# First tiles of a spectral-mixing kernel in pieces of 256 columns, the second K tile in three passes, eight warm-up products instead of nine

## The chip, the core and the metric

The kernel runs on one core of a Trainium2 chip. The metric is the device time of one execution in microseconds (us): the median before is 1849.59 us over three runs (1849.43, 1849.59 and 1850.13). Lower is better.

## What is computed

A Fourier mixing of x along both dimensions (real part only) and a token-mixing MLP on a layer-normed x are joined by a gate per token. All tensors are float32.

```python
# x: (1, 2048, 1024); DFT matrices 2048x2048 and 1024x1024, real and imaginary; F = 3584
g = sigmoid((x * gate_w).sum(-1, keepdims=True))
p, q = einsum("bsd,ed->bse", x, dft_hid_re), einsum("bsd,ed->bse", x, dft_hid_im)
a = einsum("ts,bse->bte", dft_seq_re, p) - einsum("ts,bse->bte", dft_seq_im, q)
h = layernorm(x)                                   # over the 1024 channels
u = gelu(einsum("bsd,sf->bdf", h, w1) + b1)
b = (einsum("bdf,fs->bds", u, w2) + b2).transpose(0, 2, 1)
out = g * a + (1 - g) * b
```

## The kernel before

**Stages.** Four stages follow each other, each a large matrix product: `Fourier` (names q_...), `Mixed` (y_...), `Up` (u_...) and `Down` (o_...). Each is a bilinear scheme of 26 block products, a table of plus and minus signs that says which blocks are added up before a product and where the product is added to. A block product j goes over K tiles of 128 rows. For K tile k there is a stationary tile W (q_W..., 128 rows of x by 512 columns in the first stage, 256 KB) and a moving tile R (q_R..., 128 rows of a DFT matrix by 1024 columns, 512 KB). For `Fourier` there are 4 K tiles, taken in groups of 1, 1 and 2 (`Q_TAKES`), and the product fills all eight PSUM banks: four 128-column blocks m of W by two 512-column halves n of R.

**Split operands.** Every operand is split into a rounded part `hi` (fp32r, a copy on ACT or DVE) and a rest `lo` (a subtraction on DVE), and three products stand for one: hi·hi, hi·lo and lo·hi. So one block product of `Fourier` is 4 K tiles x 8 banks x 3 = 96 matmuls of 128x128 by 128x512.

**Order.** Tasks (a load, a split, a group of matmuls, a copy out of PSUM) are entered in a `Graph`. `schedule` plays the program through with costs from a table (`HOP`, `ISSUE`, `dve`, `act`, `DMA_RATE`, `DMA_LATENCY`, and `FIRST_LATENCY` for loads whose key is below `FIRST_KEYS`), takes matmul tasks strictly in the order in which they were entered, and orders all others on ACT, DVE, SP and POOL by due time. It also picks the SBUF slot of each buffer. The program order that comes out is then fixed on every engine. A change of the costs can thus move instructions anywhere behind it, though never a matmul group before another.

**The head of the program.** The first block product (j = 0) starts from nothing. TensorE runs nine products of a constant (`warm_up`, line 1328 in the profile) while the first tiles come. In the text below W0, W1, W2, W3 and R0 to R3 are the tiles of K tiles 0 to 3 of this first block product. W0 is loaded by a DMA from ACT's queue, R0 in two halves of 512 columns and everything else from SP's queue (line 573 is the helper `load`). For K tile 0, `Fourier.split` makes W0's `hi` on ACT in two parts of 128 and 384 columns (line 990), R0's first half `hi` on DVE (line 998), W0's `lo` and the `lo` of R0's first half on DVE (line 1010), and the second half of R0 by the general helper (596 on ACT, 603 on DVE). `Fourier.matmuls` (line 1035) then goes pass by pass over four banks at a time: for n = 0 W hi·R hi, W lo·R hi, W hi·R lo, then the same for n = 1. K tile 1 and the pair of K tiles 2 and 3 use the general `Bilinear.matmuls` (lines 899, 900, 901), bank by bank: hi·hi, hi·lo and lo·hi of one bank before the next bank.

**The end.** The last bank's sum is added by DVE (line 943), stored by a DMA from SP, and the program ends when it has landed. A variant in which the last bank goes in two halves exists behind the switch `LAST_HALVES`, which is False.

Of the kernel before, what the change touches and what calls it, by code (L numbers as in the profile page):

```python
# [30 lines left out]
ISSUE = {"SP": 0.43, "ACT": 0.43, "POOL": 0.85}  # L31
DMA_RATE = 375e3
DMA_LATENCY = 5.5
FIRST_LATENCY = 2.7
FIRST_KEYS = 0.5
LANES = 8


# [214 lines left out]
Y_TAKES, U_TAKES, O_TAKES = (2, 2), (2, 2), (2, 1, 1, 1, 2)  # L253
Q_WIDE, Y_WIDE, O_WIDE = "", "WR", ""
Q_BEHIND = (1,)
QUARTERS = False
LAST_HALVES = False


class Buf:  # L260
# [85 lines left out]
class Graph:  # L346
# [3 lines left out]
    def add(self, engines, key, fn, r=(), w=(), nbytes=0):  # L350
        t = Task(len(self.tasks), key, engines, fn, nbytes)
        self.tasks.append(t)

        def parts(reg):
            b, p = reg if isinstance(reg, tuple) else (reg, None)
            t.bufs[b] = None
            return b, range(b.parts) if p is None else p if isinstance(p, tuple) else (p,)

        for reg in r:
            b, ps = parts(reg)  # L360
            for p in ps:
# [137 lines left out]
def gated_mix_kernel(  # L499
# [62 lines left out]
    def slot(n, name, dtype=F32):  # L562
        return View(Buf("f" if n > H else "h", name, None, 1, dtype), 0, n)
# [383 lines left out]
    class Fourier(Bilinear):  # L947
# [13 lines left out]

        def block(self, x_, b, j, k, key):

            if (j, k) != (0, 0):
                return super().block(x_, b, j, k, key)
            src, r = self.source(x_, b, k)
            if x_ == "W":
                b = Buf("h", f"q_W{b}_p0_0", None, 4)
                for c0, n, part in self.pieces(H):
                    load(-3, View(b, c0, n, part), src[:, c0:c0 + n], queue="ACT")  # L970
                return View(b, 0, H)
            b = Buf("f", f"q_R{b}_p0_0", None, 4)
            for c0, n, part in self.pieces(H):
                load(-3, View(b, c0, n, tuple(p // 2 for p in part[::2])), src[:, c0:c0 + n])
            load(-2, View(b, H, H, (2, 3)), src[:, H:])
            return View(b, 0, D)
# [4 lines left out]

        def split(self, x_, key, v, j, k, negate):
            if (j, k) != (0, 0):
                return super().split(x_, key, v, j, k, negate)
            if x_ == "W":
                hi, lo = Buf("h", "q_p0_w_0_hi", None, 4, F32R), slot(H, "q_p0_w_0_lo", F32R)
                for c0, n in ((0, 2 * P), (2 * P, 2 * P)) if QUARTERS else ((0, P), (P, 3 * P)):
                    part = tuple(range(c0 // P, (c0 + n) // P))
                    c, src = View(hi, c0, n, part), View(v.buf, c0, n, part)
                    g.add({"ACT": act(n)}, key - 3, lambda e, c=c, src=src: nc.scalar.activation(  # L990
                        c.ap, src.ap, AF.Copy, scale=-1.0 if negate else 1.0), r=(src.reg,), w=(c.reg,))
                self.low(key - 3, v, View(hi, 0, H), lo, negate)
                return View(hi, 0, H), lo
            both = [Buf("f", f"q_p0_r_0_{p}", None, 4, F32R) for p in ("hi", "lo")]
            for c0, n, part in self.pieces(H):
                part = tuple(p // 2 for p in part[::2])
                hi, src = View(both[0], c0, n, part), View(v.buf, c0, n, part)
                g.add({"DVE": dve(n)}, key - 3, lambda e, hi=hi, src=src: nc.vector.tensor_scalar(
                    hi.ap, src.ap, -1.0 if negate else 1.0, None, op0=ALU.mult), r=(src.reg,), w=(hi.reg,))
            first, second = [[View(b, c, H, part) for b in (v.buf, *both)] for c, part in ((0, (0, 1)), (H, (2, 3)))]  # L1000
            self.low(key - 3, *first, negate)
            split_into(key - 2, *second, negate)
            return [View(b, 0, D) for b in both]
# [9 lines left out]

        def matmuls(self, j, ks, ops, eps):

            if j or ks != (0,):
                return super().matmuls(j, ks, ops, eps)
            (rh, rl), (wh, wl) = ops[0]
            for n in range(2):
                for m in range(4):  # L1020
                    self.PS[0, m, n] = View(Buf("ps", f"ps_q_p0_{m}_{n}"), 0, H)
# [137 lines left out]
    class Down(Bilinear):  # L1159
# [46 lines left out]
        def matmuls(self, j, ks, ops, eps):  # L1206
            if not (LAST_HALVES and j == len(self.out) - 1 and ks[-1] == self.nk - 1 and ks[0]):
                return super().matmuls(j, ks, ops, eps)
            self.nm -= 1
            super().matmuls(j, ks, ops, eps)  # L1210
            self.nm += 1
            m, old = self.nm - 1, self.PS[j % self.chains, self.nm - 1, 0]
            (q, coef), = self.reads[j]
            b = self.perm[0][q // 2] * 2 + self.perm[2][q % 2]
            o, key = self.C.pop((b, m, 0)), step + len(ks) + 1
            for h in range(2):
                c, bank = slice(h * H // 2, (h + 1) * H // 2), View(old.buf, h * H // 2, H // 2, (2 * h, 2 * h + 1))

                def go(_, c=c, bank=bank):
                    for i, ((rh, rl), (wh, wl)) in enumerate(ops):  # L1220
                        for w, r in ((wh, rh), (wh, rl), (wl, rh)):
                            nc.tensor.matmul(bank.ap, w.ap[:, m * P:(m + 1) * P], r.ap[:, c], start=False,
                                             stop=(i, w) == (len(ops) - 1, wl), skip_group_check=True)

                g.add({"PE": 0.36 * len(ops)}, step, go, r=[v.reg for x in ops for pair in x for v in pair], w=(bank.reg,))
                half = View(o.buf, o.c0 + h * H // 2, H // 2, (o.part[h],))
                self.accumulate(key, b, m, 0, half, bank, eps * coef)
                _, dst, _ = self.place(b, m)
                store(key, dst[:, c], None, half, "SP")

        def finish(self, key, b, m, n, o, j):
            _, dst, reg = self.place(b, m)
# [91 lines left out]

    def warm_up(_):
        ones = nc.const_aps.tensor(1.0, [P, H], mybir.dt.bfloat16)
        for n in range(9):
            nc.tensor.matmul(pw.t, ones[:, :P], ones, start=True, stop=True)  # L1328

    g.add({"PE": 4.0}, 0, warm_up, w=(pw,))  # L1330

    for st in (Fourier(), Mixed(), Up(), Down()):
        st.build()
# [61 lines left out]
```

## Time and profile before

| | us |
|---|---|
| median of three runs | 1849.59 |
| the profiled execution | 1849.4 |
| its span, first to last instruction | 1847.6 |
| TensorE matmul busy in the span | 1842.9 |
| DVE busy | 1692.4 |
| ACT busy | 875.2 |
| first matmul of the work starts at | 4.58 |
| last matmul starts at | 1843.38 |

The span begins with the first instruction that the profile holds; 1.8 us of the time of the execution lie outside it. Rows of the timeline read: start in us, duration in us, engine, line, operation, out<-in by names without numbers, tile, count, and in brackets the idle time before it with what ended it. PE is TensorE's matmul, PEld its weight load, SPq and ACTq the DMA issues of those queues. Matmuls are pipelined: the 0.39 us of one matmul overlap the next, so the distance between starts says what one costs.

### The profile page before, as it was taken

The numbers are of one execution on the slowest core, as the hardware profiler recorded it, in microseconds if no ns is written. First come the engines' busy times: TensorE is split into PE (matmuls) and PEld (weight loads), VectorE is DVE, ScalarE is ACT, GpSimd is POOL, SyncE is SP. The second block draws the span as 40 slices with busy tenths as digits, with TensorE's granted clock in tenths as the row PEclk, the third lists the DMA queues.
The fourth block names the chain that finished last, engine by engine and source line by source line (L and its number), as shares of the span: only waits on it lengthen the run. The fifth ranks groups of instructions, "written<-read, shape, count | busy, mean of one in ns | idle before, by whom it ended". The sixth has DMA issues, their size and how long they took to land.

```text
span 1847.6 us, 23997 instructions
## 1 busy us (share of the span) xinstructions
PE 1842.9 (100%) x8121; PEld 1524.0 (82%) x8121; DVE 1692.4 (92%) x2370; ACT 875.2 (47%) x1311; POOL 206.4 (11%) x355
## 2 busy tenths in 40 slices
PE   9999999999999999999999999999999999999999
PEld 7888888888888888888888888888888888888887
DVE  8999689989989999989889798879999999999995
ACT  5533334434344786597343344444654534444441
POOL 0100010111021001001121000001220000001111
PEclk9999999999999999999999999999999999999999
DMA  9978387969698887988677447667899666674963
GB/s 379 359 249 282 126 284 295 336 244 375 240 328 313 298 297 259 354 306 288 221 255 241 163 148 254 225 210 246 295 372 295 193 211 209 214 217 114 302 166 69
DMA packets 189451, 472.71 MB, mean 256 GB/s; under 512 B 23248, under 2 KB 23248, under 8 KB 189328
## 3 DMA queue, kind: packets, MB, share of 16 engines
q1 hardware_dynamic: 156240, 368.40, 58.3%
q0 software_dynamic: 32944, 102.52, 16.7%
q8 instruction: 63, 1.03, 0.2%
q14 instruction: 60, 0.49, 0.1%
q10 hardware_dynamic: 144, 0.26, 0.0%
HBM read 367.29 MB, written 103.81 MB: 255 GB/s over the span
## 4 chain that ended last, share of the span: by engine, by line
PE 100%; DVE 0%; issue 0%
PE ps_q_p L901 10%; PE ps_q_p L900 10%; PE ps_q_p L899 10%; PE ps_o_p L901 9%; PE ps_u_p L900 9%; PE ps_u_p L901 9%; PE ps_o_p L900 9%; PE ps_o_p L899 9%; PE ps_u_p L899 9%; PE ps_y_p L899 5%; PE ps_y_p L900 5%; PE ps_y_p L901 5%; PE ps_q_p L1035 0%; PE pw L1328 0%; DVE o_c L943 0%
## 5 line engine op out<-in xcount | busy, mean ns | idle before, releaser
L899 PE MATMUL ps_o_p<-o_p_r,o_p_w 128*128 128x512 f32 x728 | 283.2, 389 | 0.0
L900 PE MATMUL ps_o_p<-o_p_r,o_p_w 128*128 128x512 f32 x728 | 283.2, 389 | 0.0
L901 PE MATMUL ps_o_p<-o_p_r,o_p_w 128*128 128x512 f32 x728 | 283.2, 389 | 0.0
L900 PE MATMUL ps_u_p<-u_p_r_lo,u_p_w_hi 128*128 128x512 f32 x595 | 231.5, 389 | 0.0
L901 PE MATMUL ps_q_p<-q_p_r_hi,q_p_w_lo 128*128 128x512 f32 x576 | 224.1, 389 | 0.0
L899 PE MATMUL ps_u_p<-u_p_r_lo,u_p_w_hi 128*128 128x512 f32 x483 | 187.9, 389 | 0.0
L901 PE MATMUL ps_u_p<-u_p_r_lo,u_p_w_lo 128*128 128x512 f32 x483 | 187.9, 389 | 0.0
L596 ACT ACTIVATE q_p_r_hi<-q_R_p 128x1024 fp32r<-128x1024 f32 (+1 forms) x100 | 103.9, 1053 | 169.1 <-DVE q_R_p L566 87.3
L596 ACT ACTIVATE u_p_w_hi<-u_W_p 128x896 fp32r<-128x896 f32 x104 | 97.1, 950 | 150.4 <-DVE u_W_p L566 75.5
L899 PE MATMUL ps_q_p<-q_p_r_hi,q_p_w_lo 128*128 128x512 f32 x416 | 161.8, 389 | 0.0
L900 PE MATMUL ps_q_p<-q_p_r_lo,q_p_w_lo 128*128 128x512 f32 x416 | 161.8, 389 | 0.0
L900 PEld LDWEIGHTS ps_o_p<-o_p_r,o_p_w 128*128 128x128 f32 x728 | 136.7, 188 | 28.5
L899 PEld LDWEIGHTS ps_o_p<-o_p_r,o_p_w 128*128 128x128 f32 x728 | 136.7, 188 | 28.3
L901 PEld LDWEIGHTS ps_o_p<-o_p_r,o_p_w 128*128 128x128 f32 x728 | 136.7, 188 | 28.3
L899 PE MATMUL ps_q_p<-q_p_r_hi,q_p_w_hi 128*128 128x512 f32 x408 | 158.7, 389 | 0.0
L900 PE MATMUL ps_q_p<-q_p_r_lo,q_p_w_hi 128*128 128x512 f32 x408 | 158.7, 389 | 0.0
L603 DVE TENSOR_TENSOR q_p_r_lo<-q_R_p,q_p_r_hi 128x1024 fp32r<-128x1024 f32 (+1 forms) x100 | 120.3, 1214 | 13.0 <-ACT q_p_r_hi L596 10.4
L900 PEld LDWEIGHTS ps_u_p<-u_p_r_lo,u_p_w_hi 128*128 128x128 f32 x595 | 111.7, 188 | 23.1
L901 PEld LDWEIGHTS ps_q_p<-q_p_r_hi,q_p_w_lo 128*128 128x128 f32 x576 | 108.1, 188 | 22.4
L943 DVE SCALAR_TENSOR_TENSOR q_c<-ps_q_p,q_c 128x512 f32<-128x512 f32 x168 | 110.1, 684 | 16.7 <-PE ps_q_p L901 12.7
L596 ACT ACTIVATE o_p_r<-o_R_p 128x512 fp32r<-128x512 f32 x113 | 70.0, 626 | 87.1 <-DVE o_R_p L569 32.0
L899 PEld LDWEIGHTS ps_u_p<-u_p_r_lo,u_p_w_hi 128*128 128x128 f32 x483 | 90.7, 188 | 18.9
(315 smaller groups left out, 4126.3 us busy)
## 6 DMA issues: line engine op xcount, KB each, us to landing
q_R_p<-in_ct_dram SPq DMA_DIRECT2D x131, 512.0 KB, 7.4
u_W_p<-in_w_dram SPq DMA_DIRECT2D x120, 448.0 KB, 4.4
o_R_p<-in_w_dram SPq DMA_DIRECT2D x110, 256.0 KB, 4.7
o_R_p<-u SPq DMA_DIRECT2D x85, 256.0 KB, 5.6
q<-q_c POOLq DMA_DIRECT2D x80, 256.0 KB, 6.3
q_W_p<-in_x_dram SPq DMA_DIRECT2D x75, 256.0 KB, 6.7
y_W_p<-q SPq DMA_DIRECT2D x75, 256.0 KB, 6.3
u<-u_c POOLq DMA_DIRECT2D x72, 256.0 KB, 4.2
```

Of the source, the lines that this page charges most:

```text
L596: g.add({"ACT": act(v.n)}, key, lambda e: nc.scalar.activation(hi.ap, v.ap, AF.Copy, scale=-1.0 if negate else 1.0), r=(v.reg,), w=(hi.reg,))
L603: nc.vector.tensor_sub(lo.ap, v.ap, hi.ap.bitcast(F32))
L899: nc.tensor.matmul(bank.ap, wh.ap[:, c], rh.ap[:, e], start=a, stop=False, skip_group_check=True)
L900: nc.tensor.matmul(bank.ap, wh.ap[:, c], rl.ap[:, e], start=False, stop=False, skip_group_check=True)
L901: nc.tensor.matmul(bank.ap, wl.ap[:, c], rh.ap[:, e], start=False, stop=b, skip_group_check=True)
L943: lambda e: nc.vector.scalar_tensor_tensor(o.ap, ps.ap, scale, o.ap, op0=ALU.mult, op1=ALU.add),
```

## The change

- `QUARTERS` becomes True: W0 is loaded in two pieces of 128x256 from ACT's queue, the first half of R0 in two pieces of 128x256 from SP's queue, and each piece has its own `hi` (ACT for W0, DVE for R0). The first of the three passes of n = 0 runs in eight products of 256 columns (banks 0 and 1 with the first 256 columns, then with the second, then banks 2 and 3 alike) in place of four of 512.
- `PASSES` is new: W1 is loaded from ACT's queue right behind W0, its key is lowered by one, and K tile 1 runs in three passes over all eight banks.
- `warm_up` runs eight products.
- The planner: loads with a key below 8 (0.5 before) count with a latency of 4.0 us (2.7 before), and a matmul task no longer depends on another matmul task.
- The variant behind `LAST_HALVES` is rewritten, and stays switched off.

```diff
-FIRST_LATENCY = 2.7
-FIRST_KEYS = 0.5
+FIRST_LATENCY = 4.0
+FIRST_KEYS = 8
...
-QUARTERS = False
+QUARTERS = True
 LAST_HALVES = False
+PASSES = True
+WARM = 8
...
         t.deps.pop(t, None)
+        if "PE" in engines:
+            t.deps = {d: None for d in t.deps if "PE" not in d.engines}
...
         def block(self, x_, b, j, k, key):
 
+            if (x_, j, k) == ("W", 0, 1) and PASSES:
+                v = slot(H, f"q_W{b}_p0_1")
+                load(-3, v, self.source(x_, b, k)[0], queue="ACT")
+                return v
...
             if (j, k) != (0, 0):
-                return super().split(x_, key, v, j, k, negate)
+                return super().split(x_, key - (PASSES and (x_, j, k) == ("W", 0, 1)), v, j, k, negate)
...
         def matmuls(self, j, ks, ops, eps):
 
+            (rh, rl), (wh, wl) = ops[0]
+            if j == 0 and ks == (1,) and PASSES:
+                banks = dict(self.PS)
+                for w, r in ((wh, rh), (wl, rh), (wh, rl)):
+                    def go(_, w=w, r=r):
+                        for n in range(2):
+                            for m in range(4):
+                                nc.tensor.matmul(banks[0, m, n].ap, w.ap[:, m * P:(m + 1) * P], r.ap[:, n * H:(n + 1) * H],
+                                                 start=False, stop=False, skip_group_check=True)
+
+                    g.add({"PE": 0.2275 * 8}, step, go, r=(w.reg, r.reg), w=[v.reg for v in self.PS.values()])
+                return
...
-        for n in range(9):
+        for n in range(WARM):
             nc.tensor.matmul(pw.t, ones[:, :P], ones, start=True, stop=True)
 
-    g.add({"PE": 4.0}, 0, warm_up, w=(pw,))
+    g.add({"PE": 0.43 * WARM}, 0, warm_up, w=(pw,))
```

What this does to the program order is shown at three places. In the names, p0 is the first block product, the number behind it the K tile, and hi and lo the two parts; the last number only tells buffers apart. Lines of the changed kernel are 4 to 21 higher.

**Place 1, the first DMA issues and ACT's first work.** SP's queue at the program's start, before and now:

```order
L573 DMA q_R8_p0_0_261<-in_ct_dram 128x512 x2
L573 DMA q_R8_p0_1_264<-in_ct_dram 128x1024
L573 DMA q_W1_p0_1_266<-in_x_dram 128x512
L573 DMA q_R8_p0_2_268<-in_ct_dram 128x1024
L573 DMA q_R8_p0_3_270<-in_ct_dram 128x1024
```

```order
L577 DMA q_R8_p0_0_260<-in_ct_dram 128x256 x2
L577 DMA q_R8_p0_0_260<-in_ct_dram 128x512
L577 DMA q_R8_p0_1_267<-in_ct_dram 128x1024
L577 DMA q_R8_p0_2_269<-in_ct_dram 128x1024
L577 DMA q_R8_p0_3_271<-in_ct_dram 128x1024
```

R0 comes in three pieces, and W1 has left SP's queue. ACT, which issues W0 and now W1 too, then makes the hi parts, before and now:

```order
L573 DMA q_W1_p0_0_259<-in_x_dram 128x512
L990 ACT_TABLE_LOAD
L990 ACTIVATE q_p0_w_0_hi_277<-q_W1_p0_0_259 128x128
L990 ACTIVATE q_p0_w_0_hi_277<-q_W1_p0_0_259 128x384
L596 ACTIVATE q_p0_r_0_hi_282<-q_R8_p0_0_261 128x512
L596 ACTIVATE q_p0_r_1_hi_316<-q_R8_p0_1_264 128x1024
L596 ACTIVATE q_p0_w_1_hi_324<-q_W1_p0_1_266 128x512
```

```order
L577 DMA q_W1_p0_0_258<-in_x_dram 128x256 x2
L577 DMA q_W1_p0_1_264<-in_x_dram 128x512
L998 ACT_TABLE_LOAD
L998 ACTIVATE q_p0_w_0_hi_278<-q_W1_p0_0_258 128x256 x2
L600 ACTIVATE q_p0_w_1_hi_298<-q_W1_p0_1_264 128x512
L600 ACTIVATE q_p0_r_0_hi_282<-q_R8_p0_0_260 128x512
L600 ACTIVATE q_p0_r_1_hi_319<-q_R8_p0_1_267 128x1024
```

The hi part of W1 moved ahead of the hi part of R0's second half.

**Place 2, TensorE at K tile 1.** Before, the first rows of K tile 1, bank by bank (the third product of a bank reads the lo part of W, which lies beside the hi part and bears its name):

```order
L899 MATMUL ps_q_p0_0_0_287<-q_p0_r_1_hi_316,q_p0_w_1_hi_324 128x512
L900 MATMUL ps_q_p0_0_0_287<-q_p0_r_1_lo_326,q_p0_w_1_hi_324 128x512
L901 MATMUL ps_q_p0_0_0_287<-q_p0_r_1_hi_316,q_p0_w_1_hi_324 128x512
L899 MATMUL ps_q_p0_0_1_306<-q_p0_r_1_hi_316,q_p0_w_1_hi_324 128x512
L900 MATMUL ps_q_p0_0_1_306<-q_p0_r_1_lo_326,q_p0_w_1_hi_324 128x512
```

Now, the first of its three passes:

```order
L1031 MATMUL ps_q_p0_0_0_285<-q_p0_r_1_hi_319,q_p0_w_1_hi_298 128x512
L1031 MATMUL ps_q_p0_1_0_286<-q_p0_r_1_hi_319,q_p0_w_1_hi_298 128x512
L1031 MATMUL ps_q_p0_2_0_294<-q_p0_r_1_hi_319,q_p0_w_1_hi_298 128x512
L1031 MATMUL ps_q_p0_3_0_295<-q_p0_r_1_hi_319,q_p0_w_1_hi_298 128x512
L1031 MATMUL ps_q_p0_0_1_321<-q_p0_r_1_hi_319,q_p0_w_1_hi_298 128x512
```

The lo part of R1 is first read by the 17th product of the K tile, where it was the second.

**Place 3, DVE at the turn from the first to the second block product.** Rows 12 to 18 of DVE's order before and now (q_c... is the sum that a PSUM bank is copied to, p1 and p2 are the next block products):

```order
L566 TENSOR_TENSOR q_R8_p0_0_261<-q_R7_p1_0_275,q_R8_p0_0_261 128x1024
L569 TENSOR_TENSOR q_W0_p1_0_314<-q_W1_p0_3_273,q_W0_p1_0_314 128x512
L603 TENSOR_TENSOR q_p2_w_0_hi_385<-q_W1_p0_3_273,q_p2_w_0_hi_385 128x512
L566 TENSOR_TENSOR q_W1_p0_0_259<-q_W0_p1_0_314,q_W1_p0_0_259 128x512
L603 TENSOR_TENSOR q_p1_r_0_lo_418<-q_R8_p0_0_261,q_p1_r_0_hi_406 128x1024
L601 SCALAR_TENSOR_TENSOR q_p1_w_0_hi_420<-q_W1_p0_0_259,q_p1_w_0_hi_420 128x512
L566 TENSOR_TENSOR q_R7_p1_1_322<-q_R7_p1_1_322,q_R4_p1_1_332 128x1024
```

```order
L570 TENSOR_TENSOR q_R8_p0_0_260<-q_R7_p1_0_276,q_R8_p0_0_260 128x1024
L573 TENSOR_TENSOR q_W0_p1_0_308<-q_W1_p0_3_274,q_W0_p1_0_308 128x512
L941 TENSOR_SCALAR q_c5_0_411<-ps_q_p0_0_0_285 128x512
L570 TENSOR_TENSOR q_W1_p0_0_258<-q_W0_p1_0_308,q_W1_p0_0_258 128x512
L607 TENSOR_TENSOR q_p1_r_0_lo_421<-q_R8_p0_0_260,q_p1_r_0_hi_401 128x1024
L570 TENSOR_TENSOR q_R7_p1_1_317<-q_R7_p1_1_317,q_R4_p1_1_335 128x1024
L605 SCALAR_TENSOR_TENSOR q_p1_w_0_lo_437<-q_W1_p0_0_258,q_p0_w_1_hi_298 128x512
```

A copy out of a PSUM bank, which ACT made before, stands on DVE where a split for the third block product stood; that split comes later, and two rows have changed places. From here to the split of W3 for the second block product both orders have 25 rows on DVE, of the same sizes.

More of the change, by code (lines that the diff above doesn't have):

```diff
@@ L1014, in matmuls @@
         def matmuls(self, j, ks, ops, eps):
+            (rh, rl), (wh, wl) = ops[0]
[9 more added lines that the diff above has]
+                return
             if j or ks != (0,):
                 return super().matmuls(j, ks, ops, eps)
-            (rh, rl), (wh, wl) = ops[0]
             for n in range(2):
@@ L1215, in matmuls, with go @@
             o, key = self.C.pop((b, m, 0)), step + len(ks) + 1
-            for h in range(2):
-                c, bank = slice(h * H // 2, (h + 1) * H // 2), View(old.buf, h * H // 2, H // 2, (2 * h, 2 * h + 1))
-                def go(_, c=c, bank=bank):
+            fresh = View(Buf("ps", "ps_o_last", None, 4), 0, H // 2, (0, 1))
+            _, dst, _ = self.place(b, m)
+            for h, bank in enumerate((View(old.buf, 0, H // 2, (0, 1)), fresh)):
+                c = slice(h * H // 2, (h + 1) * H // 2)
+                half = View(o.buf, o.c0 + h * H // 2, H // 2, (o.part[h],))
+                def go(_, c=c, bank=bank, h=h):
                     for i, ((rh, rl), (wh, wl)) in enumerate(ops):
                         for w, r in ((wh, rh), (wh, rl), (wl, rh)):
-                            nc.tensor.matmul(bank.ap, w.ap[:, m * P:(m + 1) * P], r.ap[:, c], start=False,
-                                             stop=(i, w) == (len(ops) - 1, wl), skip_group_check=True)
+                            nc.tensor.matmul(bank.ap, w.ap[:, m * P:(m + 1) * P], r.ap[:, c],
+                                             start=h == 1 and (i, w, r) == (0, wh, rh), stop=(i, w) == (len(ops) - 1, wl),
+                                             skip_group_check=True)
                 g.add({"PE": 0.36 * len(ops)}, step, go, r=[v.reg for x in ops for pair in x for v in pair], w=(bank.reg,))
[L1226 to L1229, printed above, removed]
+                self.accumulate(key + h, b, m, 0, (o, half)[h], (old, bank)[h], eps * coef)
+                store(key + h, dst[:, c], None, half, "SP")
         def finish(self, key, b, m, n, o, j):
```

## The prediction

> **What bounds the kernel now.** I read the page's first lines, then the chain that ended last, then the waits of TensorE, and last the timeline of the first 11 us.
>
> ```profile
> PE 1842.9 (100%) x8121; PEld 1524.0 (82%) x8121; DVE 1692.4 (92%) x2370; ACT 875.2 (47%) x1311; POOL 206.4 (11%) x355
> PE 100%; DVE 0%; issue 0%
> ```
>
> TensorE is busy throughout, and the chain that ended last is TensorE alone. A pipelined matmul can look busy while it waits, so I look at what its two queues waited for in the whole run:
>
> ```profile
> PE pw L1328 <- PEq L1382: 0.8, 1, 0.8
> PEld L1328 <- issue: 2.7, 8, 0.8
> PEld ps_q_p L1035 <- ACT q_p_w_hi L990: 0.9, 2, 0.7
> PEld ps_q_p L1035 <- DVE q_p_w_hi L1010: 0.2, 1, 0.2
> ```
>
> These are all waits of TensorE (columns: us in total, times, longest). Behind line 1035, K tile 0 of the first block product, there is none in 1833 us. The windows view agrees (columns: stretch, its length, busy time and count of PE, PEld, DVE, ACT, POOL, then PEclk, DMA share, GB/s):
>
> ```profile
> 4.58:10.33 5.75, 5.75 (x24) 4.51 (x25) 3.69 (x5) 3.04 (x5) 0.00 (x0) 1.00 0.94 355
> 10.33:1843.38 1833.05, 1833.05 (x8088) 1518.33 (x8087) 1687.57 (x2364) 870.47 (x1305) 206.20 (x351) 1.00 0.75 256
> ```
>
> 1833.05 us over 8087 steps is 0.2267 us a product. The 24 products of K tile 0 would take 5.44 us at that pace and took 5.75. So what an edit of the head can recover is 0.31 us of waits, plus whatever the first product can start sooner than 4.58. The tail behind 1843.38 (one DVE add and one store, 4.2 us) isn't touched, because LAST_HALVES stays False. A change by more than 0.2% (3.7 us, about what a measurement of this kernel can tell from no change) is out of reach downwards: with the 0.31 recovered, the first product would still have to start at 1.2, before any tile has landed.
>
> **The first pass of K tile 0.** The timeline of its pieces:
>
> ```profile
> 2.87 0.15 PEld L1328 LDWEIGHTS <-const-bfloat16-1.0 128*128 128x128 bf16 x1 [0.28 <-issue]
> 3.30 0.15 PEld L1328 LDWEIGHTS <-const-bfloat16-1.0 128*128 128x128 bf16 x1 [0.28 <-issue]
> 3.73 0.15 PEld L1328 LDWEIGHTS <-const-bfloat16-1.0 128*128 128x128 bf16 x1 [0.28 <-issue]
> 4.12 0.38 PE L1328 MATMUL pw<-const-bfloat16-1.0 128*128 128x512 bf16 x1
> 4.01 0.43 DVE L998 TENSOR_SCALAR q_p_r_hi<-q_R_p 128x512 fp32r<-128x512 f32 x1 [4.01 <-DMA q_R_p<-in_ct_dram]
> 4.17 0.72 ACT L990 ACTIVATE q_p_w_hi<-q_W_p 128x128 fp32r<-128x128 f32 x2 [1.71 <-DMA q_W_p<-in_x_dram]
> 4.58 2.28 PE L1035 MATMUL ps_q_p<-q_p_r_hi,q_p_w_hi 128*128 128x512 f32 x8
> 4.93 0.69 DVE L1010 TENSOR_TENSOR q_p_w_hi<-q_W_p,q_p_w_hi 128x512 fp32r<-128x512 f32 x1 [0.49 <-ACT q_p_w_hi L990]
> 5.68 0.76 PEld L1035 LDWEIGHTS ps_q_p<-q_p_r_hi,q_p_w_hi 128*128 128x128 f32 x4 [0.20 <-DVE q_p_w_hi L1010]
> 5.76 0.42 PE L1035 MATMUL ps_q_p<-q_p_r_hi,q_p_w_hi 128*128 128x512 f32 x1
> ```
>
> The second pass (W lo) starts at 5.76, 0.14 behind the end of W0's lo on DVE (4.93 + 0.69 = 5.62). From there every product follows at 0.2267. So the term is simple: **when does the second pass start now?** Later or earlier than 5.76, the rest moves with it.
>
> Warm-up: eight products leave TensorE free at 4.12, where the ninth started. That alone gains nothing, since the first real product waited for ACT and not for the ninth.
>
> Landing of the pieces. No transfer of 1 KB rows stands in the trace, so I bound it. The rates around it:
>
> ```profile
> 2.50:3.50 1.00, 1.00 (x4) 0.39 (x3) 0.00 (x0) 0.00 (x0) 0.00 (x0) 1.00 1.06 399
> 3.50:5.00 1.50, 1.41 (x6) 0.38 (x3) 0.50 (x2) 0.72 (x2) 0.00 (x0) 1.00 1.23 214
> ```
>
> While both queues carry 2 KB rows, 399 GB/s move; when SP's is alone, 214. W0 and half of R0 (512 KB) landed at 4.17 and 4.01. If small rows keep the rate, the first pieces (half the bytes, 0.66 us less at 399 GB/s) land at about 3.45 and the second ones where the whole did, 4.15. If a row of half the size takes as long as a whole one, the first pieces land where the whole did and the second 0.85 us later: the 128 KB + 128 KB that are then left take the 0.66 us of a whole, with some 0.2 for the issue; say 5.0. I take the middle, 3.6 and 4.45.
>
> ACT's hi of 256 columns:
>
> ```profile
> L990 ACT ACTIVATE q_p_w_hi<-q_W_p x2: 309/408/508, 4.2 to 4.4; 128x128 fp32r<-128x128 f32 x1, 128x384 fp32r<-128x384 f32 x1
> L1035 PEld LDWEIGHTS ps_q_p<-q_p_r_hi,q_p_w_hi x16: 186/188/190, 4.6 to 9.0; 128*128 128x128 f32 x16
> ```
>
> Between 0.31 (128 columns) and 0.51 (384): 0.41. First product: 3.6 + 0.41 + 0.1 = 4.11 (DVE's hi of R0's piece, at most 0.43, is done by 4.03), so 4.12 behind the warm-up. A product of 256 columns streams half of 0.2267, yet loads its own weights, 0.19; it costs between 0.12 and 0.227, and I take 0.21, near the load, because a load only starts with the product before it. Four of them end at 4.12 + 0.84 = 4.96. The second piece's hi is done at 4.45 + 0.41 = 4.86, so the other four run from 4.96 to 5.80. W lo: 4.88 + 0.69 + 0.14 = 5.71, ahead of TensorE. **The second pass starts at 5.80, 0.04 later than before**: what the earlier start gives, four more weight loads take. All fast: hi at 4.56, W lo at 4.58 + 0.69 + 0.14 = 5.41, gain 0.35. All slow: hi at 5.41, first product of the second half 5.5, four of 0.227, 6.41, loss 0.65.
>
> The Trainium skill, TensorE: Matmul & The Clock Gate, section LDWEIGHTS, gives columns divided by 1.2 GHz for a weight load, 107 ns for 128 columns. The row shows 188 ns for this type, so the measurement decides; by the page the pass would end at 4.96 + 4 x 0.12 and W lo would set 5.71, a gain of 0.05 in place of the loss of 0.04.
>
> **W1 by ACT's queue, K tile 1 in passes.** R0's second half and R1 arrived like this before:
>
> ```profile
> 5.33 0.63 ACT L596 ACTIVATE q_p_r_hi<-q_R_p 128x512 fp32r<-128x512 f32 x1 [0.43 <-DMA q_R_p<-in_ct_dram]
> 7.45 1.06 ACT L596 ACTIVATE q_p_r_hi<-q_R_p 128x1024 fp32r<-128x1024 f32 x1 [1.48 <-DMA q_R_p<-in_ct_dram]
> 8.41 0.61 ACT L596 ACTIVATE q_p_w_hi<-q_W_p 128x512 fp32r<-128x512 f32 x1
> 9.68 0.68 DVE L603 TENSOR_TENSOR q_p_w_hi<-q_W_p,q_p_w_hi 128x512 fp32r<-128x512 f32 x1
> 10.33 0.39 PE L899 MATMUL ps_q_p<-q_p_r_hi,q_p_w_hi 128*128 128x512 f32 x1
> ```
>
> K tile 1 started at 10.33 with no wait: W1's hi was done at 9.02, its lo at 10.36 and read at 10.79. The three passes are the same 24 products; they need R1's lo 16 products later, but nothing waited for it. Gain: 0, against 0.4 us of margin that becomes more. What is new stands on ACT: its FIFO now has W1's hi ahead of the hi of R0's second half, which n = 1 needs 8 products behind the second pass, at 5.80 + 1.81 = 7.61. ACT needs 0.61 + 0.63 + 0.1 for the two, so W1 must land by 6.3. W1 and R0's second half are 512 KB on two queues; behind 4.0 they take 1.3 us at 399 GB/s and 2.45 at 214, and the landing was some 0.5 us behind the last bytes: 5.8 or 6.95. So 0 to 0.7 us; I take 0, because two queues ran at 399. R1 hi behind it has until 10.4. Bytes up to W1 are the same as before, so K tiles 2 and 3 land as before (SP's order behind R1 only lost W1).
>
> **The plan behind.** The order moves on all engines. Where the second block product takes its last pair, DVE is nearest to being late:
>
> ```profile
> 36.10 1.28 DVE L601 SCALAR_TENSOR_TENSOR q_p_w_lo<-q_W_p,q_p_w_hi 128x512 fp32r<-128x512 f32 x2
> 38.66 0.39 PE L901 MATMUL ps_q_p<-q_p_r_hi,q_p_w_lo 128*128 128x512 f32 x1
> ```
>
> The lo of W3 is done at 37.38 and read at 38.66: 1.3 us. The same number of DVE rows of the same sizes stands ahead of it now (place 3), so the margin changes by the head's shift alone. I cost the new plan at 0: it is hidden by margins of over a microsecond. Without this cover each late microsecond is one lost, since TensorE never catches up.
>
> **Sum.** +0.04 for the first pass, and 0.1 for a part of the ACT wait: a span of 1847.7 and an execution of 1849.5. The profiled execution, 1849.4, lies 0.2 below the median of three, so the median is forecast at **1849.7 us**: no change.
>
> **Rivals.**
> 1. *The pieces pay in full*: small rows at 399 GB/s; second pass at 5.41, 1849.25 us. For it: nothing else waits. Against it: 214 GB/s right behind.
> 2. *The clock comes one window later.* The warm-up's loads are 0.43 apart, and only the product from 3.73 to 4.12 is shorter (0.39): the full clock came within the eighth product, some 3.2 us behind the first at 0.78. The clock column can't show it: it reads 1.00 already in the row 2.50:3.50. If the grant now falls behind 4.12 and TensorE idles there, another 3.3 us at 0.427 instead of 0.2267 lose 7 products, 1.6 us: 1851.3. For it: the margin is under 0.4 us. Against it: the three times before lie within 0.7. The Trainium skill, same page, section What's actually happening, has the window free-running, not started by the kernel; by that rule this can differ between executions, and the trace of one can't decide it.
> 3. *The other side: ACT blocks n = 1.* It decides when W1 lands after 6.3. If it lands as late as before (8.4 by the row at 8.41), R0's hi is done at 9.65 and n = 1 starts at 9.75, 2.1 us late: 1851.8, slower than before.
> 4. *The new plan stalls TensorE in mid-kernel by more than margin*: over 1853.3. It would take five or more DVE operations ahead of one operand.
> 5. *The change doesn't do what it says*: ruled out by the order of the changed program, which has the pieces and the passes (places 1 and 2).
>
> **How the numbers follow.** Forecast 47%, rival 1 26%, rival 2 12%, rival 3 10% (half of it under 1851.2), rival 4 4%, over 3.7 us faster 1%. Low: the full gain less the 0.2 us by which runs lie under their median, 1848.9. High: rival 2, with the slow bounds of the first pass (0.65) and ACT (0.7) inside it, 1851.3. Faster by over 0.2% 1%, within 95%, slower 4%.
>
> **What would show it.** The start of the second pass (first 512-column product of line 1054) at 5.8; the eight products 0.21 apart; ACT's hi of W1 starting before 6.3; no wait of PE or PEld behind K tile 0; the last warm-up product shorter than 0.43. A wait at n = 1, or real products 0.43 apart, would make the prediction wrong.

## The result, and the profile after

| | before | after |
|---|---|---|
| median, us (22 runs each) | 1849.71 | 1851.93 |
| lowest to highest, us | 1849.35 to 1850.32 | 1851.01 to 1854.01 |
| the profiled execution, us | 1849.4 | 1853.64 |
| its span, us | 1847.6 | 1851.8 |

The change makes the kernel slower: ratio 1.0013, interval 1.0007 to 1.0019. The after-times fall in two groups: 15 runs from 1851.01 to 1852.05 (their median is 1851.76), and 7 from 1853.26 to 1854.01. The profiled execution belongs to the upper one, so it shows one cost more than the median run has; the experiments take the two costs apart.

The engines' totals say little. TensorE, busy 1842.9 us before, now reads:

```profile
PE 1844.9 (100%) x8124; PEld 1526.3 (82%) x8124; DVE 1692.5 (91%) x2371; ACT 876.8 (47%) x1311; POOL 206.4 (11%) x355
```

Still 100%, in a span 4.2 us longer. The waits of TensorE's two queues in the whole run of the changed kernel (us in total, times, longest) say more:

```profile
PE ps_q_p L1054 <- ACT q_p_r_hi L600: 2.3, 1, 2.3
PE pw L1349 <- PEq L1403: 0.8, 1, 0.8
...
PEld ps_q_p L1054 <- ACT q_p_r_hi L600: 2.7, 1, 2.7
PEld L1349 <- issue: 2.4, 7, 0.8
PEld ps_q_p L1054 <- ACT q_p_w_hi L998: 0.6, 1, 0.6
PEld ps_q_p L1054 <- DVE q_p_w_hi L1018: 0.2, 1, 0.2
```

Before, no wait stood in K tile 0 that was longer than 0.7 us. Now one of 2.3 us (2.7 on the weight load) stands there, on ACT's `hi` of R: the first product of n = 1. The timeline of the changed kernel around it:

```profile
3.46 0.29 DVE L1006 TENSOR_SCALAR q_p_r_hi<-q_R_p 128x256 fp32r<-128x256 f32 x1 [3.46 <-DMA q_R_p<-in_ct_dram]
3.62 0.42 ACT L998 ACTIVATE q_p_w_hi<-q_W_p 128x256 fp32r<-128x256 f32 x1 [0.19 <-DMA q_W_p<-in_x_dram]
4.09 1.43 PEld L1054 LDWEIGHTS ps_q_p<-q_p_r_hi,q_p_w_hi 128*128 128x128 f32 x8 [0.64 <-ACT q_p_w_hi L998]
...
4.52 0.42 ACT L998 ACTIVATE q_p_w_hi<-q_W_p 128x256 fp32r<-128x256 f32 x1 [0.48 <-DMA q_W_p<-in_x_dram]
...
5.71 0.76 PEld L1054 LDWEIGHTS ps_q_p<-q_p_r_hi,q_p_w_hi 128*128 128x128 f32 x4 [0.19 <-DVE q_p_w_hi L1018]
...
6.75 1.08 PE L1054 MATMUL ps_q_p<-q_p_r_lo,q_p_w_hi 128*128 128x512 f32 x4
8.95 0.63 ACT L600 ACTIVATE q_p_w_hi<-q_W_p 128x512 fp32r<-128x512 f32 x1 [4.01 <-DMA q_W_p<-in_x_dram]
...
9.48 1.57 ACT L600 ACTIVATE q_p_r_hi<-q_R_p 128x512 fp32r<-128x512 f32 x2
...
10.15 2.57 PE L1054 MATMUL ps_q_p<-q_p_r_hi,q_p_w_hi 128*128 128x512 f32 x8 [2.32 <-ACT q_p_r_hi L600]
...
12.52 1.91 PE L1054 MATMUL ps_q_p<-q_p_r_lo,q_p_w_hi 128*128 128x512 f32 x4
```

The head is nearly as forecast: the pieces' `hi` start at 3.46 and 3.62, the second pass at 5.72 (forecast 5.80). Then ACT stands idle for 4.01 us until W1 comes at 8.95, makes W1's `hi`, and only at 9.48 the `hi` of R0's second half. n = 1 starts at 10.15. Its last product of the third pass of n = 0 began at 7.45, so with no wait n = 1 would have started at 7.68: **2.47 us lost**. The DMA view says why (issues of the first 3.2 us: KB each, us from issue to landing). Before:

```profile
q_R_p<-in_ct_dram SPq DMA_DIRECT2D x2, 256.0 KB, 3.7
```

This is the median of R0's two halves, which landed at 3.99 and 5.31. After:

```profile
q_R_p<-in_ct_dram SPq DMA_DIRECT2D x2, 128.0 KB, 2.9
q_R_p<-in_ct_dram SPq DMA_DIRECT2D x1, 256.0 KB, 6.9
q_W_p<-in_x_dram ACTq DMA_DIRECT2D x1, 256.0 KB, 7.3
```

R0's second half, issued at 1.65, landed at 8.54; W1, issued at 1.67, at 8.93, which is not even earlier than by SP's queue before (8.37).

The second cost stands in the windows (stretch, length, busy time and count of PE, PEld, DVE, ACT, POOL, PEclk, DMA share, GB/s):

```profile
3.50:5.00 1.50, 1.50 (x7) 0.88 (x5) 0.58 (x3) 0.83 (x2) 0.00 (x0) 1.00 0.81 138
...
7.45:10.15 2.70, 0.39 (x2) 0.00 (x0) 0.54 (x1) 1.20 (x3) 0.00 (x0) 1.00 1.01 410
...
11.60:15.05 3.45, 3.45 (x9) 2.64 (x9) 3.38 (x4) 2.77 (x4) 0.00 (x0) 0.51 1.02 401
15.05:1847.65 1832.60, 1832.60 (x8086) 1518.50 (x8085) 1684.71 (x2361) 869.39 (x1301) 206.21 (x351) 1.00 0.75 255
```

From 11.60 to 15.05 the granted clock is 0.51: eight products, each 0.427 us behind the last instead of 0.2267 (in the timeline, four products in 1.91 us from 12.52, where four took 1.08 from 6.75). That is 8 x 0.20 = **1.6 us lost**. Behind 15.05 it is 1832.60 over 8086 steps, 0.2266 us a product, as before. The sum: -0.04 (second pass), 2.47, 1.6, and some 0.2 in the first steps behind the two waits (0.34 instead of 0.23), 4.2 us in all, the difference of the spans. Row 3.50:5.00 moved 138 GB/s where the kernel before moved 214 (its row stands in the prediction): in this stretch R0's second half fell behind.

### The profile page after: what moved, and what is told of

It reads as the page before. It is cut to its first block, busy times and chain, and to the rows that moved or that the text cites. A ratio compares the mean times of both kernels' runs of the same rounds, so it can differ in the third digit from the quotient of the medians.

```text
span 1851.8 us, 24015 instructions
## 1 busy us (share of the span) xinstructions
PE 1844.9 (100%) x8124; PEld 1526.3 (82%) x8124; DVE 1692.5 (91%) x2371; ACT 876.8 (47%) x1311; POOL 206.4 (11%) x355
## 4 chain that ended last, share of the span: by engine, by line
PE 99%; DMA 0%; ACT 0%; ACTq 0%; DVE 0%; issue 0%
PE ps_q_p L904 10%; PE ps_q_p L905 10%; PE ps_q_p L903 10%; PE ps_o_p L904 9%; PE ps_u_p L904 9%; PE ps_u_p L903 9%; PE ps_o_p L905 9%; PE ps_u_p L905 9%; PE ps_o_p L903 9%; PE ps_y_p L905 5%; PE ps_y_p L903 5%; PE ps_y_p L904 5%; DMA q_W_p<-in_x_dram 0%; PE ps_q_p L1031 0%; PE ps_q_p L1054 0%; ACTq L577 0%
## 5 line engine op out<-in xcount | busy, mean ns | idle before, releaser
L905 PE MATMUL ps_q_p<-q_p_r_hi,q_p_w_lo 128*128 128x512 f32 x728 | 283.6, 390 | 0.0
L904 PE MATMUL ps_u_p<-u_p_r_lo,u_p_w_hi 128*128 128x512 f32 x588 | 229.0, 389 | 0.0
L903 PE MATMUL ps_q_p<-q_p_r_hi,q_p_w_lo 128*128 128x512 f32 x584 | 227.4, 389 | 0.0
L904 PE MATMUL ps_q_p<-q_p_r_lo,q_p_w_lo 128*128 128x512 f32 x584 | 227.4, 389 | 0.0
L903 PE MATMUL ps_u_p<-u_p_r_lo,u_p_w_hi 128*128 128x512 f32 x504 | 196.3, 390 | 0.0
L905 PE MATMUL ps_u_p<-u_p_r_lo,u_p_w_lo 128*128 128x512 f32 x504 | 196.3, 390 | 0.0
L905 PEld LDWEIGHTS ps_q_p<-q_p_r_hi,q_p_w_lo 128*128 128x128 f32 x728 | 136.7, 188 | 28.3
L903 PEld LDWEIGHTS ps_q_p<-q_p_r_hi,q_p_w_lo 128*128 128x128 f32 x584 | 109.7, 188 | 22.8
L904 PEld LDWEIGHTS ps_q_p<-q_p_r_lo,q_p_w_lo 128*128 128x128 f32 x584 | 109.7, 188 | 22.6
```

What stands on the lines that cost most here:

```text
L903: nc.tensor.matmul(bank.ap, wh.ap[:, c], rh.ap[:, e], start=a, stop=False, skip_group_check=True)
L904: nc.tensor.matmul(bank.ap, wh.ap[:, c], rl.ap[:, e], start=False, stop=False, skip_group_check=True)
L905: nc.tensor.matmul(bank.ap, wl.ap[:, c], rh.ap[:, e], start=False, stop=b, skip_group_check=True)
```

## The experiments

Theory A at the outset: W1 on ACT's queue delays R0's second half, and ACT's order adds to it; TensorE's idle time then brings the half clock. The rivals are the pieces, the warm-up and the early start.

**1. W1 back on SP's queue**, pieces, passes and warm-up as in the change.

```diff
-            if (x_, j, k) == ("W", 0, 1) and PASSES:
-                v = slot(H, f"q_W{b}_p0_1")
-                load(-3, v, self.source(x_, b, k)[0], queue="ACT")
-                return v
```

> Edit: the changed kernel with W1 back on SP's queue behind R1; pieces, the three passes and eight warm-up products stay. Theory A (W1 on ACT's queue is what makes R0's second half late): R0's second half lands before 5.8 (8.5 in the changed kernel), n = 1 starts without a wait, no product at half clock; 1849.4 to 1849.8 us. Theory B (the small pieces with their extra DMAs make it late): it still lands after 7.5, a wait of over 1 us stays; 1850.8 to 1852. Theory C (only the order on ACT costs): landing as in the changed kernel, about 8.5, but ACT makes R0's hi at once, so the wait shrinks to about 1.5 us; 1851.

Measured: 1849.59 us (1849.11 to 1850.02), ratio 1.0000, interval 0.9990 to 1.0009. The whole loss is gone, as theory A asks. The timeline of this run:

```profile
7.20 0.63 ACT L600 ACTIVATE q_p_r_hi<-q_R_p 128x512 fp32r<-128x512 f32 x1 [2.51 <-DMA q_R_p<-in_ct_dram]
...
7.88 2.09 PE L1050 MATMUL ps_q_p<-q_p_r_hi,q_p_w_hi 128*128 128x512 f32 x8 [0.28 <-ACT q_p_r_hi L600]
```

But R0's second half still landed at 7.18, between the two theories' landings (before 5.8, after 7.5) and not at the 5.31 of the kernel before, though W1 now stood behind it. n = 1 waited 0.45 us, of which the earlier second pass (5.47) paid back 0.29. So the landing is late in this trace without W1 ahead of it, too.

**2. No pieces**, W1 stays on ACT's queue.

```diff
-QUARTERS = True
+QUARTERS = False
```

> Edit: the changed kernel with the pieces undone (W0 and R0's first half whole, line 1054 in products of 512 columns); W1 stays on ACT's queue, the passes and eight warm-up products stay. Theory A: W1 shares the 16 engines with R0's second half, which lands 1.5 us or more later than the 5.3 of the kernel before; a wait before n = 1 of over 0.5 us; 1850.3 to 1852. Theory B: both land by 6.3, no wait; 1849.5 to 1849.9.

Measured: 1849.90 us (nine runs from 1849.69 to 1850.02, one at 1851.74), ratio 1.0002, interval 0.9992 to 1.0012: theory B's time. R0's second half landed at 6.31, W1 at 6.56; ACT, whose order has W1 first, began the two `hi` at 6.58 and 7.12:

```profile
6.58 0.63 ACT L600 ACTIVATE q_p_w_hi<-q_W_p 128x512 fp32r<-128x512 f32 x1 [1.74 <-DMA q_W_p<-in_x_dram]
...
7.12 1.78 ACT L600 ACTIVATE q_p_r_hi<-q_R_p 128x512 fp32r<-128x512 f32 x2
...
7.79 2.11 PE L1054 MATMUL ps_q_p<-q_p_r_hi,q_p_w_hi 128*128 128x512 f32 x8
```

n = 1 started at 7.79 with almost no wait (0.06 us). Neither half of the change costs anything that shows in the median; together they cost 2.2 us. The reason is a margin. Before, the `hi` of R0's second half was done at 5.96 and needed at 7.61: 1.65 us. W1 on ACT alone takes 1.0 (landing) and 0.8 (ACT reached it at 7.12, not at 6.31) of it, the pieces alone 1.9 (landing) in experiment 1. Each fits, or nearly. In the changed kernel's profile the landing is 3.2 later and ACT's order takes 0.9: 4.1 less 1.65 is about the wait of 2.47.

**3. ACT's order**: the changed kernel with the `hi` of R0's second half ahead of W1's.

```diff
...
+                    g.add({"ACT": act(H)}, key, lambda e: nc.scalar.activation(
+                        hi.ap, v.ap, AF.Copy, scale=-1.0 if negate else 1.0), r=(v.reg, self.second.reg), w=(hi.reg,))
...
+            self.second = second[1]
```

The `hi` of W1 now also reads (`r=`) the `hi` of R0's second half, so it can't be made before it.

> Edit: the changed kernel with one order more in the plan: ACT makes the hi part of R0's second half before the hi part of W1 (W1 stays on ACT's queue). Theory C (the order on ACT is the whole cost): no wait before n = 1; 1849.5. Theories A and B (the landing is late): R0's second half still lands near 8.5, its hi is done near 9.2 in place of 10.1, the wait falls from 2.5 to about 1.5 us; 1850.7 to 1851.2, and half clock is rarer or gone.

Measured: 1850.74 us (1850.26 to 1853.09), ratio 1.0007, interval 0.9998 to 1.0016: 1.2 us under the changed kernel, over half of its loss. The profiled execution is the highest of the ten, the only one over 1851.3, with both costs (landing at 8.99, a wait of 2.15 us, half clock from 10.71 to 14.12):

```profile
9.01 0.63 ACT L600 ACTIVATE q_p_r_hi<-q_R_p 128x512 fp32r<-128x512 f32 x1 [4.18 <-DMA q_R_p<-in_ct_dram]
9.54 0.62 ACT L994 ACTIVATE q_p_w_hi<-q_W_p 128x512 fp32r<-128x512 f32 x1
...
9.69 2.94 PE L1061 MATMUL ps_q_p<-q_p_r_hi,q_p_w_hi 128*128 128x512 f32 x8 [1.99 <-ACT q_p_r_hi L600]
```

So the new order takes away ACT's part of the loss and not the late landing.

**4. Nine warm-up products** in the changed kernel.

```diff
-WARM = 8
+WARM = 9
```

> Edit: the changed kernel with nine warm-up products. If the missing ninth product costs the clock (rival 2 of the prediction), the upper group of times (1853.3 to 1854.0) disappears and all runs lie near 1851.8. If the half clock comes from the idle time before n = 1, nothing changes: times of 1851.0 to 1854.0 as in the changed kernel, the first product 0 to 0.3 us later.

Measured: 1851.35 us (1850.95 to 1853.43), ratio 1.0011, interval 1.0001 to 1.0020. The loss stays, and one run of ten lies in the upper group; the ninth product doesn't prevent it (whether it makes it rarer, ten runs can't tell). In the profiled execution R0's second half landed at 7.22, W1 at 8.00; TensorE waited 1.36 us and kept the full clock.

**5. TensorE kept busy**: the changed kernel with ten more products of the constant ahead of n = 1, into a bank that n = 1 starts anew.

```diff
+                if n == 1:
+                    def filler(_, bank=self.PS[0, 0, 1]):
+                        ones = nc.const_aps.tensor(1.0, [P, H], mybir.dt.bfloat16)
+                        for _ in range(10):
+                            nc.tensor.matmul(bank.ap, ones[:, :P], ones, start=True, stop=True, skip_group_check=True)
+
+                    g.add({"PE": 2.2}, step, filler, w=(self.PS[0, 0, 1].reg,))
```

> Ten more products of the constant stand between the last pass of n = 0 and the first of n = 1, into a bank that n = 1 starts anew, so TensorE is busy for some 2.2 us of the time in which the changed kernel waits. Theory A (the half clock behind the wait, products 0.426 us apart for 3.4 us, is set off by TensorE standing idle before n = 1): no product of the work 0.4 us apart, none of the runs over 1852.5, where 7 of 22 of the changed kernel lie above 1853.2; the rest as the changed kernel's lower group or up to 0.5 us above it, 1851.0 to 1852.0, since the operand sets the start of n = 1 and not the products. Theory B (the half clock comes from the earlier start of the work or from the shorter warm-up): the upper group stays at about a third of the runs, near 1853.5.

Measured: 1851.94 us (1851.63 to 1852.51 in 11 runs), ratio 1.0012, interval 1.0003 to 1.0021. None of the 11 runs lies in the upper group (1853.26 and more), where the changed kernel's share, 7 of 22, would put three or four; theory A asks for that. Its timeline:

```profile
7.45 2.36 PE L1045 MATMUL ps_q_p<-const-bfloat16-1.0 128*128 128x512 bf16 x10
9.23 0.63 ACT L600 ACTIVATE q_p_w_hi<-q_W_p 128x512 fp32r<-128x512 f32 x1 [4.59 <-DMA q_W_p<-in_x_dram]
...
10.44 2.11 PE L1061 MATMUL ps_q_p<-q_p_r_hi,q_p_w_hi 128*128 128x512 f32 x8 [0.63 <-ACT q_p_r_hi L600]
...
12.38 0.84 PE L1061 MATMUL ps_q_p<-q_p_r_lo,q_p_w_hi 128*128 128x512 f32 x3
```

The operand came even later (n = 1 at 10.44), and the span was 1850.5, 1.3 us less than that of the changed kernel's profile. The useful work waited as long; only the half clock is gone (eight products in 2.11 us and three in 0.84, against eight in 2.57 and four in 1.91). So the two costs are separate, and the second hangs on TensorE's idle time.

**6. Pieces by rows**: two transfers of 64x512 each for W0 and for R0's first half.

```diff
...
+                    for p in (0, P // 2):
+                        q.dma_start(v.ap[p:p + P // 2, :], src[p:p + P // 2])
...
```

> W0 and the first half of R0 still come in two transfers each, but cut by rows (64 rows of 512 columns, 2 KB a row) and not by columns (128 rows of 256, 1 KB a row). The hi parts stay in pieces, and each now needs both transfers. Theory A (what delays R0's second half is the number of transfers ahead of it): it lands between 7.2 and 9.0 as in the runs with pieces and W1 on ACT's queue; a wait of over 1 us before n = 1 and a median of 1851 to 1852.5. Theory B (it is the 1 KB rows): it lands near 6.3 as without pieces, with almost no wait, 1849.6 to 1850.3. In both the first product starts later than 4.09, near 4.6.

Measured: 1855.02 us (1853.53 to 1856.48), ratio 1.0028, interval 1.0018 to 1.0038. Inconclusive on its question: R0's second half landed at 7.38, within theory A's range, but it was issued 0.6 us later (a 64-row issue took 0.56 to 0.84 us, a 128-row one in the changed kernel 0.38 to 0.45); from issue to landing it took 5.1 us, as without pieces in experiment 2. The second piece of R0's first half came only at 5.91, and ACT's table load, begun at 4.76, ended at 6.04, so the wait (2.5 us) moved into the first pass; behind it the half clock ran from 6.94 to 10.36.

**7 and 8. Pieces of one operand alone**, W1 on ACT's queue: R0's first half whole (7), or W0 whole (8). The edit replaces `self.pieces(H)` in one of the two loads:

```diff
-            for c0, n, part in self.pieces(H):
+            for c0, n, part in [(0, H, (0, 1, 2, 3))]:
```

> Pieces for W0 alone: R0's first half comes in one transfer; W1 stays on ACT's queue. In this order ACT makes the hi of R0's second half ahead of the hi of W1. Theory A (each transfer ahead, on either queue, costs the second half of R0 some 0.5 to 1 us): it lands near 7.2, between 6.3 without pieces and 7.2 to 9.0 with both; n = 1 waits some 0.3 to 0.5 us; 1849.8 to 1850.5. Theory B (only R0's own pieces, ahead of it on the same queue, delay it): it lands near 6.3, no wait, 1849.3 to 1849.9.

> Pieces for R0 alone: W0 comes in one transfer on ACT's queue, with W1 behind it; ACT makes the hi of W1 ahead of the hi of R0's second half as in the changed kernel. Theory A (each transfer ahead, on either queue): R0's second half lands near 7.2, W1 near 7.5, n = 1 waits about 1 us; 1850.3 to 1851.3. Theory B (R0's own pieces alone): it lands as with both, 7.2 to 9.0, with a wait of 1.4 to 2.5 us; 1851 to 1852.5.

Measured, 7: 1850.94 us (1850.70 to 1853.30), ratio 1.0010, interval 1.0001 to 1.0019. R0's second half landed at 5.59, nearer to theory B; but W0's second piece came at 5.77, and TensorE waited 1.4 us for it in the first pass. Measured, 8: 1851.35 us (five runs from 1850.25 to 1850.74, five from 1851.96 to 1852.32), ratio 1.0009, interval 1.0000 to 1.0018. R0's second half landed at 7.19, the second piece of its first half at 4.97, W1 at 5.25. The profiled execution is one of the upper five: TensorE waited 0.44 us for that second piece, the full clock came only at 9.37, and the second pass began at 7.12, so n = 1 found its operand ready. In both, the second piece of the one operand that is cut lands later (5.77 and 4.97) than with both cut (4.2 to 4.7 for W0, 4.0 to 4.4 for R0's first half), and the cost falls in the first pass. Neither theory foresaw that.

**9. No passes**: the changed kernel with `PASSES = False`, which also puts W1 back on SP's queue, in the same order of transfers as in experiment 1.

> The changed kernel without its passes: K tile 1 goes bank by bank again and W1 is back on SP's queue, the pieces stay. Its first transfers are those of the run that only put W1 back on SP's queue. Theory A (the passes themselves are worth nothing): R0's second half lands near 7.2 as there, n = 1 waits under 0.6 us, one time between 1849.0 and 1850.3. Rival (the passes gave margin that is now missing): a wait of TensorE at K tile 1, behind R1's lo, of over 0.3 us.

One run: 1849.33 us. No wait at n = 1 (7.66) and none at K tile 1: in this execution nothing is lost without the passes. They need not be quite worthless: with the landings of experiment 1, W1's lo was done at 11.40 and K tile 1 began at 10.73, so that bank by bank its third product, due at 11.18, would have waited; an estimate from these times is 0.3 us. R0's second half landed at 5.92, where experiment 1 with the same transfers had 7.18: between executions this landing varies by more than a microsecond.

**10. R0's second half in two transfers**, in the kernel before.

```diff
-            load(-2, View(b, H, H, (2, 3)), src[:, H:])
+            for c0, part in ((H, 2), (H + H // 2, 3)):
+                load(-2, View(b, c0, H // 2, (part,)), src[:, c0:c0 + H // 2])
```

> The kernel before, with R0's second half in two transfers of 128x256 instead of one of 128x512; nothing else. Theory A (a transfer whose first packets start between some 3.5 and 5 us gets a few of them at 0.5 to 1.9 us, whatever it is; SP's third transfer is the one): the second piece, now SP's third, lands at 6.3 or later where the whole half landed at 5.31, and R1, now begun later, no later than before, 7.4. Rival (it takes cut pieces ahead of the half, the half itself being cut does nothing): both pieces land by 5.6.

One run: 1849.50 us; the pieces landed at 5.30 and 5.71, close to the rival's 5.6, against 5.31 for the whole. That SP's third transfer is always the late one is refuted.

**11. Everything later**: five memsets by DVE ahead of the first loads of the kernel before.

```diff
+        for b in t.need:
+            if b.name.startswith("q_") and b.name.endswith("_p0_0") and b.name[2] in "WR":
+                for _ in range(4 if b.name[2] == "W" else 1):
+                    nc.vector.memset(b.t[:, :H], 0.0)
```

> The kernel before, with five DVE memsets of W0's and R0's buffers ahead of their loads, so that all first loads are issued some 1.5 to 2 us later. Theory A (the slow stretch belongs to the transfers: it comes when the first ones are through): the rate falls as before some 2.7 us behind the first issue, that is in 5.0 to 7.0, and R0's second half lands some 4.1 us behind its issue. Rival (the slow stretch belongs to the time since the program's start, 3.5 to 5.7): the rate of the first transfers is low at once, below 250 GB/s in 3.8 to 5.2, and from 5.75 on it is full, so that R0's second half lands less than 4 us behind its issue and no slow stretch follows.

W0 was issued at 3.41, R0 from 3.95 on, 2.7 and 3.2 us later than before. One run, 1854.12 us. Its windows:

```profile
3.50:5.00 1.50, 1.26 (x3) 0.15 (x1) 0.42 (x1) 1.19 (x1) 0.00 (x0) 1.00 0.30 106
5.00:6.50 1.50, 0.00 (x0) 0.00 (x0) 0.00 (x0) 0.52 (x3) 0.00 (x0) 1.00 0.95 310
6.50:8.00 1.50, 0.11 (x1) 0.14 (x2) 0.69 (x2) 0.32 (x2) 0.00 (x0) 1.00 1.07 242
8.00:9.50 1.50, 1.50 (x4) 1.22 (x5) 1.50 (x3) 0.61 (x1) 0.00 (x0) 0.51 0.89 294
```

The low stretch is no longer at 3.5 to 5.7: 310 GB/s first, then 242, though the dip is shallower than before (214). R0's second half took 3.6 us from issue (4.1 before), which is on the rival's side, R1 5.7 (5.8 before). Single packets say it more clearly: R1's first ones, which took up to 1.86 us in the kernel before, from 4.17 on, took up to 1.85 us here, from 6.57 on. So the slow stretch goes with the transfers and not with the time since the start; the size of the dip isn't settled by one run.

**12. W0's pieces alone, W1 on SP's queue** (the edits of experiments 1 and 7 together), a version that might beat both.

> The changed kernel with W1 back on SP's queue and R0's first half in one transfer: of the pieces only W0's two are left, and the passes. Theory A (R0's own pieces push its second half into the slow stretch, W0's on the other queue do not): R0's second half lands at 5.3 to 6.0, n = 1 waits for nothing, the second pass starts between 5.5 and 5.8, 1849.3 to 1849.8: at best 0.3 us under the kernel before, which the interval cannot tell from no change. Rival (any piece ahead delays it): it lands at 6.5 to 7.2, a wait up to 0.5 us, 1849.6 to 1850.3.

Measured: 1850.98 us (seven runs from 1850.80 to 1851.13, four from 1852.10 to 1853.38), ratio 1.0010, interval 1.0001 to 1.0019: slower, for a reason that no theory had. In the profiled execution, one of the four, R0's second half landed at 5.53 as theory A said, but W0's second piece only at 5.78:

```profile
4.15 0.42 ACT L994 ACTIVATE q_p_w_hi<-q_W_p 128x256 fp32r<-128x256 f32 x1 [1.20 <-DMA q_W_p<-in_x_dram]
...
5.80 0.42 ACT L994 ACTIVATE q_p_w_hi<-q_W_p 128x256 fp32r<-128x256 f32 x1 [1.24 <-DMA q_W_p<-in_x_dram]
...
9.00 1.42 PE L1050 MATMUL ps_q_p<-q_p_r_lo,q_p_w_hi 128*128 128x512 f32 x4
```

The first piece came as late as whole W0 had (4.15), the second 1.65 us later; TensorE waited 0.64 us for it and kept the start's half clock until 9.70 (four products in 1.42 us instead of 1.08). That the break kept the full clock away, here and in experiment 8, is an inference from two traces.

No version beats the kernel before by more than the interval.

## Why the prediction was wrong

**Bounds: right.** Behind the head nothing waits, and the end moves with the head.

**Warm-up: right.** Nine products change nothing that shows (experiment 4).

**First pass: right in its sum, in part by luck.** Landings 3.43 and 3.60, then 4.23 and 4.50, were taken as 3.6 and 4.45; `hi` 0.42 us, taken 0.41; the second pass at 5.72, taken 5.80. The reason given for a product of 256 columns was wrong: its load's 0.19 is no floor. Under the half clock the steps were 0.21 (4.47, 4.69, 4.90), the price taken, for another reason; under the full clock 0.12 (5.22, 5.33, 5.45), less than its own load's 0.19, since the loads overlapped there (they start 0.12 apart). So TensorE was done before W0's lo (4.97 + 0.69 = 5.66) and waited 0.2 us for it, where the forecast had TensorE set the second pass; the prediction's other reckoning, products of 0.12 and W lo setting 5.71, is what came. The gain stayed small all the same: in the executions with both operands in pieces the full clock came at 3.8 to 5.6 us and W0's second piece landed at 4.2 to 4.7, and the second pass started anywhere from 5.47 (experiment 1) to 5.90 (experiment 4), against 5.76.

**W1 by ACT's queue: this step failed.** The prediction said that W1 and R0's second half "take 1.3 us at 399 GB/s and 2.45 at 214", and "I take 0, because two queues ran at 399". The row 3.50:5.00 with 214 GB/s had been read as one queue running alone. It is a slow stretch that comes with one queue or two: 138 GB/s in the changed kernel, 194 in experiment 1, 186 in experiment 2, 212 in 7 and 8. W1 landed at 8.93, not at 5.8 or 6.95, and R0's second half, for which the prediction took no delay from the pieces at all, at 8.54 instead of 5.31. The other end of the sum, 0.7 us at 214 GB/s, would have been too little as well. Of the 2.47 us, 0.9 come from ACT's order (the half had landed at 8.54, and ACT took it up at 9.48), the rest from the landing. A margin of 1.65 us was weighed against one part of the change only, while two drew on it.

**Rival 3 was half of the right mechanism** (W1 late, ACT's queue blocking n = 1), and its 1851.8 us is what the lower group shows (1851.76). That the number fits so well is partly luck: it had R0's second half in time, and with ACT's order mended (experiment 3) 1.2 us of loss stay. It was given 10%, half of that under 1851.2, and so the range ended below it, at 1851.3. The low bound doesn't follow from its words either: 1849.25 less 0.2 is 1849.05, not 1848.9; nothing hangs on it.

**The half clock was missing** as a consequence of a wait. Rival 2 had it at the start only, where the changed kernel's trace doesn't show it (full clock at 4.78) but experiments 8 and 12 do. It adds 1.6 us to the wait in the profiled execution; the group of 7 runs in 22 to which that one belongs lies 1.8 us above the other, and experiment 5 has no such group. The Trainium skill, TensorE: Matmul & The Clock Gate, section What's actually happening, has a free-running window of about 3.4 us: the trace agrees, the half clock lasts 3.41 us, and runs of one kernel differ. By the same section the clock falls back after an idle window of about 3.4 us; here 2.5 us of idle time were enough, so the measurement decides.

The clock of these traces changes in steps of 3.41 us. It became full at 4.78, fell two steps later at 11.61 and rose again at 15.02; in experiment 3 the times are 3.88, 10.71 and 14.12, in experiment 6 3.53, 6.94 and 10.36. In the step that ended with the fall TensorE had been idle for 1.95 us (of the 2.47, in 8.20 to 11.61), in experiment 3 for 2.15, in 6 for 2.5, in 11 for 3.1; 1.36 us in one step (experiment 4) and 1.42 (experiment 7) brought no fall. If the idle time within one step decides, which these traces allow but don't show, the same wait costs the clock or not by where it lies. Whether the 15 runs of the lower group escaped by that or by a shorter wait stays open, since the one trace of the changed kernel is of the upper group.

**The plan and the passes: right**, no gain or loss that shows in the times (experiments 1 and 9).

**What stays open:** why the transfers that start behind some first 500 KB are slow, in nearly every kernel here and the one before too, and why the landing varies by a microsecond and more between executions (R0's second half with both edits: 8.54, 8.99, 7.22 and 8.33). It is later than the 5.31 of the kernel before in every trace with one edit (6.31 with W1 on ACT's queue; 7.18 and 5.92 with the pieces), and with both later still; with one or two traces each, what either edit adds isn't settled, and the mechanism in the DMA engines isn't shown.

## What to carry to other kernels

At the start of a program read each operand's margin (done against needed), and charge every edit that shifts its landing to that one margin together, not edit by edit. A rate in one row isn't explained by which queues happen to be active: ask whether a second kernel with other queues shows the same row. A wait of 2 us and more on TensorE cost its length and, in some runs, a slow stretch behind it, so a wait that can't be avoided may be filled with products that write to a bank not yet in use, though here the fill only took away the upper group of times.

## What the hardware showed beside it

- **A dip behind the first transfers.** In the kernel before, the changed one and all but two of the experiments (6 and 11, whose loads are cut by rows or held back) the rate falls from 295 to 399 GB/s in 2.5 to 3.5 us to 82 to 242 in 3.5 to 5.0. Packets of 2 KB mostly took 84 ns and of 4 KB 159 ns; in the dip the first ones of R0's second half took up to 1.4 us in the changed kernel, and those of R1 up to 1.86 us in the kernel before.
- **Cutting a first transfer made the other landings later.** The Trainium skill, Perfetto Trace Analysis, section DMA Optimizations, says that smaller chunks may let the whole complete sooner if the DMA engines are generally idle. Here they weren't (share 1.04 and 1.06 in 2.50 to 3.50, after and before), and the first pieces came 0.55 us sooner in the changed kernel while R0's second half came 0.6 us (experiment 9) and 1.9 us (experiment 1) later with the pieces alone. The first 1.5 MB (W0, R0, R1 and W1) had all landed at 8.48 to 10.27 in the six traces with both operands cut by columns, at 7.82 to 8.53 in the seven others whose loads began as early.
- **Idle time and the clock.** After one wait of 2.47, 2.15 (experiment 3), 2.5 (experiment 6) or 3.1 us (experiment 11) the half clock came for 3.41 us; after 1.36 (experiment 4) and 1.42 (experiment 7) it didn't.
